# Loading three quarters of w_ch by partitions 0 to 118 and 119 to 127

## The chip, the cores and the metric

The kernel runs on one core of one Trainium2 chip. The metric is the device time of one execution in microseconds (us). The time before is the median of three runs; the profile comes from one further execution of the same kernel.

## The reference

Forgetting attention over 8 batches and 8 heads (576 positions, 64 values per head), followed by a spectral mix of its output over 64 modes and a channel mix:

```python
scores = scale * q @ k.T                                  # per batch and head
decay  = cum[:, :, :, None] - cum[:, :, None, :]          # cum = cumsum(log(clip(f)))
attn   = softmax(where(causal, -1e9, scores + decay))
x      = (attn @ v).transpose(0, 2, 1, 3).reshape(B, S, 512)

X  = np.fft.rfft(x, axis=1)                               # the first 64 modes are kept
Yr = einsum('bmd,mde->bme', Xr, w_r) - einsum('bmd,mde->bme', Xi, w_i)
Yi = einsum('bmd,mde->bme', Xr, w_i) + einsum('bmd,mde->bme', Xi, w_r)
y  = np.fft.irfft(Yr + 1j * Yi, n=S, axis=1)
u  = x + y
out = u + np.maximum(u @ w_ch, 0.0)
```

The inputs w_r and w_i are 64 x 512 x 512 in float32, 134 MB together; w_ch is 512 x 512 in float32, 1 MB.

## The kernel before, in words

The kernel has two parts, in an order written out by hand (the program order of each engine is the order of the Python statements).

The first part is the attention. A loop over 32 pairs (two heads of one batch each) turns q and k with TensorE, computes scores, masks, multiplies by v, normalises into the tile `x_all`, and takes the first 64 modes by matrix multiplication (`dft`). From the tenth pair on, each step also does one or two early portions of the spectral mix (`spec_early`) with weight tiles that are already there.

The second part begins at about 230 us. It loops over 16 groups of four modes (`u`) and the remaining row blocks (`dc`) of the weights. `spec_mms` (matmuls on L194) consumes one weight tile of 1024 KB or 512 KB at a time, `fold_modes` and `fold` (L703 to L742) bring the result back to positions, and `xw` (L690) multiplies by w_ch. After the last weight tile a closing loop (L648, L854, L902, L908) adds, applies the maximum and stores the output through SP.

Nearly all loads are issued by GpSimd (POOL) and cast from float32 to bfloat16 on the way: q and k (`load_qk`, L109, 144 KB each at the destination), v (`load_v`, L119, 288 KB, not cast), the weights (`issue_w`, L156 with 512 KB and L165 with 1024 KB) and w_ch (L322, 512 KB). They share one software queue, q0. In each pair of the first part POOL issues in a fixed order: q and k of the pair four ahead, half a weight tile, v of the pair three ahead, and usually another half of a weight tile. The weight tiles have seven buffers (`wpool`), and some early ones are lent space in `x_all` and `yx` (`guests`), so in the second part a load is issued when TensorE has consumed the tile that lay in its buffer.

The program gives the software loads eight completion counters in turn. A load waits until the load eight places before it has landed, so at most eight are in flight.

The tile `wch` has 128 partitions by 4 blocks by 512 columns. It is loaded once, in `setup_late`, which is called in pair 2; its place in POOL's order is behind the load of half a weight tile on L156 and ahead of q and k of pair 7. Its first reader is L690 at 251.8 us.

Of the kernel before, what the change touches and what calls it, by code (L numbers as in the profile page):

```python
# [17 lines left out]
def _strided(ap: bass.AP, free_dims, offset_elems: int = 0) -> bass.AP:  # L18
    new_ap = [list(ap.ap[0])] + [list(x) for x in free_dims]
    return bass.AP(tensor=ap.tensor, offset=ap.offset + offset_elems, ap=new_ap)  # L20
# [3 lines left out]
def kernel(  # L24
# [11 lines left out]
    nc = tc.nc  # L36
# [32 lines left out]
    wch = const.tile([128, NEB, D], BF16, name="wch")  # L69
# [245 lines left out]
    def setup_late():  # L315
        nc.vector.memset(XS[:, :, 24 * NM : XROW], 0.0)
        nc.vector.tensor_copy(
            perm[:].rearrange("p (b j ri) -> p b j ri", b=8, j=4),
            ident_bf[:].rearrange("p (j x ri b) -> p b j x ri", j=4, x=2, ri=2)[:, :, :, 0, :],
        )  # L320
        nc.vector.tensor_copy(rep[:], _strided(ident_bf[:, KF:128], [[0, 4], [1, KL]]))
        nc.gpsimd.dma_start(wch[:], moe_w_ch.rearrange("(eb p) e -> p eb e", p=128))  # L322

    def setup_bi(sc):
        ns = SBLK[sc]
# [226 lines left out]
    for i in range(NPAIR + 2):  # L552
# [56 lines left out]
        if i == 2:  # L609
            setup_late()  # L610
# [12 lines left out]
    with ExitStack() as bctx:  # L623
# [259 lines left out]
        for i in range(len(steps)):  # L883
# [12 lines left out]
            p, sb = steps[i][0]  # L896
# [58 lines left out]
```

## Time and profile before

| | |
|---|---|
| median of three runs | 439.38 us (439.35 to 440.37) |
| the profiled execution's own time | 440.52 us |
| its span in the profile | 438.7 us |
| mean granted TensorE clock | 0.936 |
| TensorE matmul busy | 346.3 us (79%) |
| VectorE busy | 268.2 us (61%) |
| ScalarE busy | 235.8 us (54%) |
| GpSimd busy | 133.6 us (30%) |
| bytes written by DMA | 96.75 MB, mean 221 GB/s |
| HBM read | 163.73 MB |
| the w_ch load: issue, to landing | at 32.3 us, 13.1 us |

Busy time is the time that an engine spent in instructions; it says nothing on whether the end waited for them. The chain of work that ended last, followed back from the last instruction, tells that. A "DMA" piece in it runs from the issue of a load to its landing, so it holds the time in which the load stood in its queue. The chip has 16 DMA engines that share the loads of a core, and a load has landed when the last of them has finished its part: its completion counter takes sixteen increments, whose times the trace keeps one by one.

### The profile page before, as it was taken

The page shows a single profiled execution, that of the slowest core. Times are in us where ns is not written, and L with a number is a line of the kernel's source. Part 1 is how long each engine was busy: PE and PEld are TensorE (multiplying, and loading weights), DVE is VectorE, ACT ScalarE, POOL GpSimd, SP SyncE. Part 2 cuts the span into 40 slices and gives each one's busy share as a digit, 9 for nine tenths or more (in the row PEclk, how much of TensorE's full clock was granted, in tenths as well). Part 3 has the DMA queues.
Part 4 walks back from the last instruction along what each step waited for, and adds up shares of the span by engine and source line. Part 5 has one row for each costly group of instructions (what it writes and reads, how often), then busy time and mean ns, then how long its engine had stood idle before and what let it go on. Part 6 is the DMA issues. An engine that isn't in the chain of part 4 may idle for free.

```text
span 438.7 us, 10283 instructions
## 1 busy us (share of the span) xinstructions
PE 346.3 (79%) x4285; PEld 189.7 (43%) x4285; DVE 268.2 (61%) x644; ACT 235.8 (54%) x360; POOL 133.6 (30%) x202
## 2 busy tenths in 40 slices
PE   1678787889888889888893594698986688989994
PEld 1455555555555565555551241343443233335231
DVE  6688889777877778888872221223132255465774
ACT  5657777778778666665640032033222355464874
POOL 6544444444454444444222111112021221100111
PEclk9999999999999999999997598599699699799999
DMA  9999999999999999999999999999999999994688
GB/s 192 205 234 219 230 220 230 231 227 229 233 230 223 230 223 230 223 229 224 234 212 212 212 212 212 212 211 212 212 212 211 210 209 209 211 210 83 249 299 316
DMA packets 68381, 96.75 MB, mean 221 GB/s; under 512 B 3568, under 2 KB 45040, under 8 KB 68336
## 3 DMA queue, kind: packets, MB, share of 16 engines
q0 software_dynamic: 62800, 85.64, 105.4%
q1 hardware_dynamic: 5536, 10.47, 6.6%
q8 instruction: 33, 0.54, 0.4%
q14 instruction: 12, 0.10, 0.1%
HBM read 163.73 MB, written 9.44 MB: 395 GB/s over the span
## 4 chain that ended last, share of the span: by engine, by line
DMA 39%; PE 33%; DVE 19%; ACT 4%; issue 3%; POOL 1%; DVEq 0%; POOLq 0%; ACTq 0%
DMA w<-in_moe_w_i_dram 22%; DMA w<-in_moe_w_r_dram 15%; DVE vT L384 5%; DVE x_all L492 4%; DVE qkT L360 4%; PE pav L477 4%; PE A L194 4%; PE sps L432 3%; PE tv L382 3%; PE pd L521 3%; PE vp L393 2%; PE U L648 2%; DMA qk<-in_k_dram 2%; PE Z L648 2%; DVE vn L372 2%
## 5 line engine op out<-in xcount | busy, mean ns | idle before, releaser
L439 ACT ACTIVATE et<-sps 128x1024 bf16<-128x1024 f32 x96 | 96.0, 1050 | 12.1 <-PE sps L432 9.7
L477 PE MATMUL pav<-vs,et 128*128 128x65 bf16 (+1 forms) x896 | 51.1, 196 | 0.2 <-DVE vn L372 0.2
L360 DVE COPY qkT<-tp 128x640 bf16<-128x640 bf16 x64 | 48.8, 763 | 2.5 <-PE tp L355 2.5
L804 DVE TENSOR_TENSOR Yb<-A,yx 128x512 bf16<-128x512 f32 x15 | 10.4, 691 | 64.5 <-PE A L194 64.5
L477 PEld LDWEIGHTS <-et 128*128 128x128 bf16 (+1 forms) x896 | 36.4, 101 | 17.2 <-issue 13.3
L194 PE MATMUL A<-w,XP 128*16 128x512 bf16 (+1 forms) x240 | 22.6, 457 | 25.7 <-DMA w<-in_moe_w_i_dram 15.4
L690 PE MATMUL pxw<-wch,xT 128*128 128x512 bf16 (+1 forms) x160 | 40.1, 405 | 0.0
L432 PE MATMUL sps<-qkT 64*128 64x512 bf16 (+4 forms) x320 | 38.9, 306 | 1.1 <-DVE qkT L360 1.1
L492 DVE TENSOR_TENSOR x_all<-pav,rcp 128x384 bf16<-128x384 f32 (+2 forms) x96 | 36.2, 377 | 3.3
L355 PE MATMUL tp<-ident_bf,qk 128*64 128x128 bf16 x576 | 29.3, 231 | 9.0 <-DMA qk<-in_k_dram 9.0
L384 DVE COPY vT<-tv 128x576 bf16<-128x576 bf16 x32 | 24.2, 758 | 19.2 <-PE tv L382 19.2
L697 ACT CAST XW<-pxw 128x512 bf16<-128x512 f32 (+1 forms) x16 | 9.4, 585 | 48.8 <-PE pxw L690 48.8
L156 POOL DMA_DIRECT2D w<-in_moe_w_r_dram x27 | 20.5, 759 | 40.7 <-PE A L194 9.3
L165 POOL DMA_DIRECT2D w<-in_moe_w_r_dram x16 | 11.9, 743 | 68.5 <-PE A L194 51.3
L404 ACT COPY vs<-vp 128x576 bf16<-128x576 bf16 x32 | 20.5, 640 | 21.4 <-PE vp L400 21.4
L697 ACT CAST yx<-pxw 128x512 bf16<-128x512 f32 (+1 forms) x24 | 14.0, 585 | 32.8 <-PE pxw L690 32.8
L165 POOL DMA_DIRECT2D w<-in_moe_w_i_dram x19 | 13.3, 699 | 54.8 <-PE A L194 26.3
L737 ACT CAST x_all<-pu 128x512 bf16<-128x512 f32 (+1 forms) x40 | 23.4, 585 | 12.0 <-PE pu L736 11.1
L109 POOL DMA_DIRECT2D qk<-in_q_dram x32 | 19.5, 611 | 31.8 <-PE sps L432 8.5
L491 DVE RECIPROCAL rcp<-pav 128x6 f32<-128x6 f32 (+2 forms) x96 | 16.2, 169 | 15.9 <-PE pav L477 15.8
L156 POOL DMA_DIRECT2D w<-in_moe_w_i_dram x27 | 20.3, 753 | 17.4 <-DMA w<-in_moe_w_i_dram 7.8
L372 DVE TENSOR_TENSOR vn<-vt,wn 128x576 bf16<-128x576 f32 x32 | 23.8, 745 | 2.3 <-ACT wn L297 2.3
(147 smaller groups left out, 669.9 us busy)
## 6 DMA issues: line engine op xcount, KB each, us to landing
w<-in_moe_w_r_dram POOLq DMA_DIRECT2D x16, 1024.0 KB, 29.6
w<-in_moe_w_i_dram POOLq DMA_DIRECT2D x15, 1024.0 KB, 32.4
w<-in_moe_w_r_dram POOLq DMA_DIRECT2D x27, 512.0 KB, 11.0
w<-in_moe_w_i_dram POOLq DMA_DIRECT2D x27, 512.0 KB, 12.3
vt<-in_v_dram POOLq DMA_DIRECT2D x29, 288.0 KB, 10.4
out_dram<-o_sb SPq DMA_DIRECT2D x10, 512.0 KB, 3.2
qk<-in_q_dram POOLq DMA_DIRECT2D x32, 144.0 KB, 10.9
qk<-in_k_dram POOLq DMA_DIRECT2D x32, 144.0 KB, 10.4
```

Source lines behind the costliest of these rows:

```text
L156: nc.gpsimd.dma_start(w8[:, t, :, :], src[4 * u : 4 * u + 4, dc * 128 : (dc + 1) * 128, :].rearrange("m p e -> p m e"),)
L165: nc.gpsimd.dma_start(w8[:, j : j + step, :, :].rearrange("p m r e -> p m (r e)"), src[m : m + step, 256:512, :].rearrange("m (p r) e -> p ...
L194: nc.tensor.matmul(A[32 * j : 32 * j + M, :], lhsT=lhsT, rhs=rhs, start=st_, stop=sp_)
L355: nc.tensor.transpose(tp[64 * hp : 64 * hp + 64, r - r0, :, :].rearrange("p n c -> p (n c)"), qk[:, hp, r * 64 : r * 64 + 64], ident_bf[:, :],
L360: nc.vector.tensor_copy(st[i]["T"][:].rearrange("p n (c r) -> p n c r", r=9)[:, :, :, r0:r1], tp[:, 0 : r1 - r0, :, :].rearrange("p r n c ...
L372: nc.vector.tensor_tensor(vn[:], st[i]["vt"][:], _strided(wn[:, widx(i), :], [[1, 9], [0, Dh]]), ALU.mult)
L384: nc.vector.tensor_copy(st[i]["vT"][:].rearrange("p (c r) -> p c r", r=9), tv[:].rearrange("p r c -> p c r"))
L432: nc.tensor.matmul(ps[:, hp, c : c + n], lhsT=KT[sl, jb * 128 : jb * 128 + 128], rhs=QT[sl, i0 : i0 + n], start=True, stop=True,)
L439: nc.scalar.activation(st[i]["et"][:, T, :, :], ps[:], ACT.Exp, scale=scale)
L477: nc.tensor.matmul(pav[:Ms, sb % 3, hp, :], lhsT=eblk(i, hp, jb, sb), rhs=rhs, start=(jb == 0), stop=(jb == sb),)
L492: nc.vector.tensor_tensor(x_all[:ns, g, b, lo:hi, :].rearrange("p s (h d) -> p s h d", h=2), pav[:ns, lo % 3 : lo % 3 + n, :, 0:Dh], _stri ...
L690: nc.tensor.matmul(pxw[rows, :], lhsT=xT[:, eb, sb * 128 : sb * 128 + Ms], rhs=wch[:, eb, :], start=(eb == 0), stop=(eb == NEB - 1),)
```

## The change

The block 0 of w_ch (a quarter) is loaded by one transfer of 128 partitions. The blocks 1 to 3 are loaded by two transfers, one of partitions 0 to 118 and one of partitions 119 to 127. All three are issued by GpSimd, at the place of the one before. The bytes are the same.

```diff
-        nc.gpsimd.dma_start(wch[:], moe_w_ch.rearrange("(eb p) e -> p eb e", p=128))
+        wrows = moe_w_ch.rearrange("(eb p) e -> p eb e", p=128)
+        for p0, p1, e0, e1 in ((0, 128, 0, 1), (0, 119, 1, 4), (119, 128, 1, 4)):
+            nc.gpsimd.dma_start(wch[p0:p1, e0:e1, :], wrows[p0:p1, e0:e1, :])
```

Everything else stands in the same order on every engine. As there are two more software loads, each later load uses the counter two places further on, and still waits for the load eight places before it.

## The prediction

> **What bounds the kernel now.** I first read the chain of work that ended last, in order of time, to see where the loads are on the path.
>
> ```profile
> by line: DMA w<-in_moe_w_i_dram 21.9%; DMA w<-in_moe_w_r_dram 15.1%; DVE vT L384 4.6%; DVE x_all L492 4.5%; DVE qkT L360 4.5%; PE pav L477 4.1%; PE A L194 3.7%; PE sps L432 2.9%; PE tv L382 2.9%; issue 2.8%; PE pd L521 2.7%; PE vp L393 2.4%
> ...
> 202.56 10.71 DMA w<-in_moe_w_r_dram
> 213.32 2.41 issue
> 215.74 22.35 DMA w<-in_moe_w_r_dram
> 238.13 1.13 PE A L194 x6
> 239.54 33.40 DMA w<-in_moe_w_i_dram
> ...
> 342.73 29.45 DMA w<-in_moe_w_i_dram
> 372.21 0.74 PE A L194 x6
> ```
>
> Up to 202 us the path runs over the computing engines. From there to 372.2 us it is weight loads, with one us of matmul between the landing of a tile and the issue of the next one into its buffer. Behind 372.2 us no load is on it.
>
> Next, stretches of the trace (columns: PE, PEld, DVE, ACT, POOL busy, granted clock, DMA share, GB/s written), to see whether the DMA engines ever run out of work.
>
> ```profile
> 42.00:45.00 3.00, 2.29 (x56) 1.77 (x57) 2.66 (x7) 2.37 (x4) 0.77 (x1) 1.00 1.23 206
> ...
> 372.00:378.00 6.00, 4.99 (x25) 2.27 (x25) 1.50 (x3) 1.75 (x3) 1.48 (x3) 0.55 1.17 212
> 378.00:384.00 6.00, 5.71 (x31) 2.12 (x29) 3.03 (x5) 3.65 (x7) 0.67 (x2) 0.88 1.14 210
> 390.00:396.00 6.00, 5.12 (x63) 2.44 (x61) 4.86 (x8) 2.58 (x6) 0.00 (x0) 1.00 1.14 211
> 396.00:399.00 3.00, 2.71 (x13) 1.19 (x12) 1.24 (x2) 2.24 (x5) 0.00 (x0) 1.00 0.76 143
> 399.00:402.00 3.00, 3.00 (x57) 2.09 (x54) 1.47 (x4) 0.94 (x2) 0.00 (x0) 1.00 0.43 79
> 402.00:405.00 3.00, 2.62 (x28) 1.38 (x28) 1.64 (x4) 1.02 (x3) 0.00 (x0) 1.00 0.00 0
> ```
>
> The share stays above 1 until 396 us (packets overlap) and then fades over six us: the sixteen engines do not end together. The times of the sixteen increments of a load's counter show the same. For the tile that lands at 372.17 us they lie, from the first,
>
> ```
> 0  0.20 0.26 0.35 0.67 1.38 2.03 | 3.19 3.45 3.90 4.78 5.25 5.45 5.63 5.76 5.80 us
> ```
>
> and this pattern hardly moves from tile to tile. So each DMA engine works through its own backlog without a pause, a delay that one of them once had is never made good, and a tile counts as landed when the latest engine is done. Seven engines are within 2.1 us of the first, nine are over 3.1 us behind. When the w_ch load landed (45.44 us) all were within 1.93 us. The delay grows in steps of about 1 us, on one engine at a time (4.62 to 5.69 us at the back between the tiles landing at 227.18 and 233.15 us). The DMA queues name what fits that:
>
> ```profile
> q0 software_dynamic: 62800, 85.64, 105.4%
> q1 hardware_dynamic: 5536, 10.47, 6.6%
> q8 instruction: 33, 0.54, 0.4%
> q14 instruction: 12, 0.10, 0.1%
> ```
>
> 33 instruction fetches of 16 KB took 0.4% x 16 x 438.7 / 33 = 0.85 us each. Their durations repeat with period eight, so I take it that eight engines carry them in turn, four times each by 398 us.
>
> Last, the matmul that waits for the tile landing at 372.17 us, in the order of time on PE:
>
> ```profile
> 370.03 0.65 PE L194 MATMUL A<-w,XP 128*16 128x512 bf16 x8
> 372.21 0.70 PE L194 MATMUL A<-w,XP 128*16 128x512 bf16 x8 [1.53 <-DMA w<-in_moe_w_i_dram]
> ```
>
> **The change, part by part.**
>
> *Two more issues on POOL.* At 0.75 us for the old load and 0.56 us for the small v load, the two add 1.1 to 1.5 us to an engine that is busy 30%. Cost nothing, unless POOL's order holds others up, which is next.
>
> *Waits moved.* The 119-partition load must wait for v landing at 32.76 us, the 9-partition load for the half tile landing at 35.88 us. Behind them on POOL stand q and k of pair 7 (issued at 33.29 and 36.17 us), half a weight tile (37.13) and v (38.05); they now wait for landings at 36.84, 37.49, 39.36 and 40.04 us, so they go out 1.5 to 4 us later. Who needs them: pair 7 is first turned at 55.3 us, and k landed at 46.73 us. Landing two to three us later leaves five us or more. Cost nothing on PE.
>
> *Backlog.* Three of the eight places are held by w_ch, two of them with little in them, so the backlog shrinks from about 11 us (32.34 to 43.51 us at the first engine) to 7 or 8 us for some ten loads. If an engine runs dry there, it loses that time for good. The engines with little work of w_ch are the first ones to. I count a pause of 0 to 1 us on some of them around 46 us; it costs only if it meets an engine that is later among the last. I take nothing for the forecast and keep 1 us for the range.
>
> *The bytes, engine by engine.* This is the part that can show. The old load was 2.55 us on every engine (524 KB at 206 GB/s; the first increments give 43.51 - 40.92 = 2.59 us), so three quarters are 1.91 us for 8 partitions, 0.24 us for each. No load in the trace has other than 64 or 128 partitions, both dealt equally over sixteen. Equal shares of 119 = 7 x 17 exist only on seven engines (or one), of 9 on nine. The seven then do 17 instead of 8 partitions, 9 x 0.24 = 2.2 us more, and the nine do 1 instead of 8, 1.7 us less. Dealt out in turn, the nine are the engines that the seven are not.
>
> On this the DMA page of the Trainium skill (DMA: Bandwidth & Descriptors, section "Why a DMA increments its semaphore by 16 and not by 1") gives the same deal: the largest count up to 16 that divides the slowest dimension, on consecutive engines from a cursor that goes round. No run shown so far tests it.
>
> *What it does to the end.* Which seven? If they are the early ones, the early group ends at 2.03 + 2.2 = 4.2 us and the late one at 5.80 - 1.7 = 4.1 us, so every tile of the last hundred us lands 5.8 - 4.2 = 1.6 us sooner. If a late engine is among the seven, its tiles land 2.2 us later. These are the two ends, -1.6 and +2.2 us, before PE has its say.
>
> PE's say: at 372.21 us PE had waited 1.53 us. Its work before reaches back without another load wait to 342.24 us, where it waited 4.21 us, so that starts 1.6 us sooner as well; about half of this is lost because the clock is at half there until 348.8 us. PE then still waits about 0.8 us at the new 370.6 us. The work behind it starts 1.6 us sooner at a full clock (the clock drops at 372.7 us) and nothing waits for a load up to the end; the last tile lands at 402.26 us against its use at 403.4 us, and both move. So the end moves by 1.6 us.
>
> **Forecast:** the profiled execution had 440.52 us, of which the span is 438.7; 1.6 us less is 438.9. The median of the three runs is 1.14 us below the profiled one, and I take the step off that: 439.38 - 1.6 = 437.8 us. A measurement of this kernel tells about 0.3% (1.3 us) from no change.
>
> **The rivals.**
>
> *The late engines get the 119 (slower).* The trace does not name engines. If the fetches lie on the half that the 119-partition load begins with, at least one engine with 5.2 to 5.8 us of delay takes 2.2 us more. The tile at 372.17 us lands at 374.3. From 372.7 to 379.5 us the clock is at half (0.55 in the stretch from 372), so a wait there costs half of itself: 1.3 us if the clock keeps its times, 2.2 us if it moves along, 440.7 to 441.6, say 441.2 us. It decides as soon as any engine over 4 us behind is among the seven. For it: a consecutive block of seven that misses all nine late ones has only one place. Against: the late ones are nine and the early ones seven, which is just the split of a deal in turn if eight engines with fetches and one neighbour are its second part. I judge 58 to 22 between these, and it is a judgement.
>
> *The 119 go out as eight per engine (no change).* Fourteen engines keep 8, one has 7, one none, and the 9 go singly to nine engines: nine engines +0.24 us, one -1.9 us. The latest engine moves by 0 to +0.24 us unless it is the one relieved, and the next (5.76 us) is 0.04 us behind it: 439.4 us, within 0.3 us. For it: it keeps all sixteen busy as every row of the trace does. Chance 0.13.
>
> By the same section of the Trainium skill some direct copies from GpSimd are dealt just so, rounded up over sixteen engines, and no row here tells whether a casting load is one of these.
>
> *An engine of the second group runs dry (less gain).* The gain falls from 1.6 to about 0.6 us, 438.8 us. For it: the smaller backlog above. Against: the early engines had a lead of 5 us on 11 us of backlog at 200 us and did not run dry. Chance 0.07.
>
> **How the numbers follow.** Forecast 0.58, slower rival 0.22, even deal 0.13, dry engine 0.07. The forecast's own range is 437.0 to 438.5 us (a step of the clock's timing is worth some 0.8 us either way); 0.05 of it lies within 0.3%. The even deal may relieve a late engine that leads the pack (0.02), the dry engine may lose less (0.03). So faster 0.58 - 0.05 + 0.02 + 0.03 = 0.58; within 0.3% 0.05 + 0.11 + 0.04 = 0.20; slower 0.22. The range of 8 in 10 reaches from the forecast's low side to the middle of the slower rival, 436.8 to 441.2 us.
>
> **What would show it.** Right: sixteen increments of late tiles within some 4.3 us instead of 5.8, DMA share fading over 4 us, the last tile landing 1.6 us sooner, the matmul of 372.21 us at about 370.6. Wrong: a pattern with one engine at 7 us or more and the same matmul near 374 us (late engines took the 119); the old pattern (even deal); a DMA share below 1.1 around 46 us (dry); q or k of pair 7 waited for at 55 us (my cover failed).

## The result and the profile after

The changed kernel takes 441.63 us (median of seven runs, 440.87 to 444.19) against 439.67 us of the kernel before (median of seven runs, 439.35 to 440.37). The ratio is 1.0042, with a 95% interval of 1.0024 to 1.0059: 1.0 to 2.6 us slower, where 1.6 us faster was forecast. The profiled execution took 441.34 us, with a span of 439.6 us; that of before took 440.52 us, above its own median, so the two profiles differ by less than the medians do.

First the page of the kernel after, the chain that ended last, by engine and by line.

```profile
DMA 42%; PE 28%; DVE 19%; issue 6%; ACT 3%; POOL 1%; DVEq 0%; POOLq 0%
DMA w<-in_moe_w_r_dram 26%; DMA w<-in_moe_w_i_dram 12%; DVE vT L386 5%; DVE x_all L494 4%; DVE qkT L362 4%; PE pav L479 4%; PE A L194 3%; PE sps L434 3%; PE tv L384 3%; PE pd L523 3%; DMA vt<-in_v_dram 3%; PE vp L395 2%; DVE vn L374 2%; DMA qk<-in_k_dram 2%; PE Z L650 2%
```

The weights are still the largest item. The same chain in order of time (start, length, what) shows a difference at its end.

```profile
354.75 29.45 DMA w<-in_moe_w_r_dram
384.48 19.72 DMA w<-in_moe_w_i_dram
405.42 0.86 PE pywl L876 x4
```

Before, the last load on the path landed at 372.2 us. Now the very last tile is on it: issued at 384.48, landed at 404.19 us. PE in order of time (start, length, and in brackets the idle time with what ended it) shows both places.

```profile
371.71 0.65 PE L194 MATMUL A<-w,XP 128*16 128x512 bf16 x8
374.20 0.66 PE L194 MATMUL A<-w,XP 128*16 128x512 bf16 x8 [1.84 <-DMA w<-in_moe_w_i_dram]
...
404.24 0.40 PE L211 MATMUL AT<-XP,w 128*128 128x16 bf16 x8 [0.40 <-DMA w<-in_moe_w_i_dram]
```

The matmul of 372.21 us starts at 374.20, which the prediction named as the sign that late engines took the 119 partitions. Next the stretches at the end (columns as before: PE, PEld, DVE, ACT, POOL, clock, DMA share, GB/s).

```profile
372.00:378.00 6.00, 3.08 (x32) 1.41 (x25) 1.70 (x3) 1.64 (x4) 1.08 (x2) 1.00 1.19 210
...
396.00:399.00 3.00, 2.71 (x13) 1.04 (x11) 1.48 (x3) 2.23 (x5) 0.00 (x0) 1.00 1.06 199
399.00:402.00 3.00, 2.86 (x54) 1.82 (x53) 1.25 (x3) 0.72 (x2) 0.00 (x0) 1.00 0.59 109
402.00:405.00 3.00, 2.24 (x26) 0.88 (x22) 1.44 (x4) 0.61 (x2) 0.00 (x0) 1.00 0.13 24
```

From 396 us on the DMA shares are close to those of two us earlier in the kernel before (1.05, 0.67 and 0.23 in 394:397, 397:400 and 400:403). The increments of the last tile tell it more exactly: the first came 1.93 and the last 1.94 us later, so the fading of the engines moved back as a whole and kept its length. The granted clock in 372 to 378 us is 1.00, against 0.55 before, so PE made up there for part of the late tile in this execution. The matmul on the last tile started at 403.37 us before and starts at 404.24 us now; these 0.87 us are the difference of the two spans (439.6 against 438.7 us).

The same view around the w_ch loads, and below it one stretch of the kernel before.

```profile
42.00:45.00 3.00, 2.29 (x58) 1.67 (x55) 2.66 (x6) 2.78 (x3) 1.10 (x2) 1.00 1.24 201
45.00:48.00 3.00, 2.53 (x32) 1.73 (x31) 2.38 (x11) 1.56 (x4) 0.11 (x1) 1.00 1.23 222
48.00:51.00 3.00, 2.64 (x63) 1.80 (x60) 2.66 (x7) 2.82 (x4) 2.59 (x4) 1.00 0.93 164
51.00:54.00 3.00, 2.18 (x26) 1.50 (x25) 2.40 (x9) 1.51 (x4) 1.81 (x4) 1.00 1.16 223
```

```profile
48.00:51.00 3.00, 2.17 (x54) 1.67 (x55) 2.66 (x7) 2.63 (x3) 0.60 (x1) 1.00 1.21 216
```

In one stretch the share falls to 0.93 and the rate to 164 GB/s, against 1.21 and 216: some engines ran dry. What held the loads up is in POOL's order of time.

```profile
32.89 0.54 POOL L324 DMA_DIRECT2D wch<-in_moe_w_ch_dram  x1 [1.72 <-DMA x_all<-in_moe_w_i_dram]
33.58 1.07 POOL L324 DMA_DIRECT2D wch<-in_moe_w_ch_dram  x1 [0.15 <-issue]
36.48 0.60 POOL L324 DMA_DIRECT2D wch<-in_moe_w_ch_dram  x1 [1.82 <-DMA w<-in_moe_w_r_dram]
...
44.50 0.60 POOL L109 DMA_DIRECT2D qk<-in_k_dram  x1 [0.35 <-DMA wch<-in_moe_w_ch_dram]
48.41 0.75 POOL L156 DMA_DIRECT2D w<-in_moe_w_r_dram  x1 [3.31 <-DMA wch<-in_moe_w_ch_dram]
```

Eight places behind the 119-partition load stands half a weight tile. It waits 3.31 us for that load and is issued at 48.41 us. In the kernel before it was issued at 42.82 us, after another wait:

```profile
42.82 0.77 POOL L156 DMA_DIRECT2D w<-in_moe_w_r_dram  x1 [1.73 <-DMA yx<-in_moe_w_r_dram]
```

Last, the sixteen increments, from the first, of the 119-partition load (42.23 to 48.13 us) and of the tile that lands at 374.16 us:

```
119 partitions   0 .03 .27 .30 .34 .34 .65 2.18 2.42 | 3.47 3.69 3.70 3.73 3.95 4.12 5.90 us
tile at 374.16   0 .12 .19 .92 1.35 1.76 1.91 | 2.91 2.95 3.01 3.08 3.13 4.42 5.65 5.85 5.89 us
```

Seven engines stand out in the first row. The second row is as wide as before (5.89 against 5.80 us), but its first increment is 1.89 us and its last 1.99 us later.

### The profile page after: what moved, and what is told of

It is laid out like the page before. It is cut to its first block, busy times and chain, and to the rows that moved or that the text cites. A ratio compares the mean times of both kernels' runs of the same rounds, so it can differ in the third digit from the quotient of the medians.

```text
span 439.6 us, 10285 instructions
## 1 busy us (share of the span) xinstructions
PE 342.9 (78%) x4285; PEld 188.3 (43%) x4285; DVE 267.9 (61%) x644; ACT 235.8 (54%) x360; POOL 134.8 (31%) x204
## 4 chain that ended last, share of the span: by engine, by line
DMA 42%; PE 28%; DVE 19%; issue 6%; ACT 3%; POOL 1%; DVEq 0%; POOLq 0%
DMA w<-in_moe_w_r_dram 26%; DMA w<-in_moe_w_i_dram 12%; DVE vT L386 5%; DVE x_all L494 4%; DVE qkT L362 4%; PE pav L479 4%; PE A L194 3%; PE sps L434 3%; PE tv L384 3%; PE pd L523 3%; DMA vt<-in_v_dram 3%; PE vp L395 2%; DVE vn L374 2%; DMA qk<-in_k_dram 2%; PE Z L650 2%
## 5 line engine op out<-in xcount | busy, mean ns | idle before, releaser
L165 POOL DMA_DIRECT2D w<-in_moe_w_i_dram x19 | 13.3, 698 | 55.9 <-PE A L194 38.2
L109 POOL DMA_DIRECT2D qk<-in_k_dram x32 | 19.6, 611 | 21.7 <-DMA w<-in_moe_w_i_dram 6.8
```

The lines of the kernel that those rows point to most:

```text
L109: nc.gpsimd.dma_start(qk[64 * n : 64 * n + 64, :, :], src[b, 2 * g : 2 * g + 2, :, :].rearrange("h (p r) d -> p h (r d)", p=64),)
L165: nc.gpsimd.dma_start(w8[:, j : j + step, :, :].rearrange("p m r e -> p m (r e)"), src[m : m + step, 256:512, :].rearrange("m (p r) e -> p ...
```

## The experiments

Three theories were open. By the first, three loads in place of one cost the time: their issues, their waits, their places among the eight in flight. By the second, the uneven deal costs it, because engines that are late anyway are among the seven heavy ones. By the third, the engines that ran dry cost it. The heavy engines of a load were read off its increments: that choice of seven out of sixteen which, with one common delay for the seven, turns the increments of the load before into those of the load after best. The number seven is not put in: in each of the nine kernels with two or three blocks of 119 partitions, six or eight heavy engines fit worse (root mean square error 0.17 to 0.39 us) than seven (0.03 to 0.15 us). An engine is called late below when it stands over 2.5 us behind the first one.

**Three loads, dealt evenly.** 112 and 16 partitions in place of 119 and 9.

```diff
-        for p0, p1, e0, e1 in ((0, 128, 0, 1), (0, 119, 1, 4), (119, 128, 1, 4)):
+        for p0, p1, e0, e1 in ((0, 128, 0, 1), (0, 112, 1, 4), (112, 128, 1, 4)):
```

> Blocks 1 to 3 of w_ch are split at partition 112 instead of 119 (112 = 16 x 7 and 16 = 16 x 1), so there are still three loads on the same three places, but equal shares exist on all sixteen DMA engines. Theory A (the 119 partitions go to seven engines; the load eight places behind waits for the slowest of them and the other nine run dry): no uneven load, no dry spell, the increments of the second load lie within 2.5 us of each other instead of 5.9, the time is that of the kernel before, 439.4 to 440.0 us. Theory B (only the deal counts: a late engine is among the seven): the same, 439.4 to 440.0 us. Theory C (three places in the window of eight instead of one are what costs): as slow as the changed kernel, 441 to 442 us.

Measured 439.6 us (12 runs; the kernel before, measured with it, 439.77 us), ratio 0.9996, interval 0.9984 to 1.0008. No seven engines stand out: the increments of the second load lie within 1.69 us. The half tile eight places behind it went out at 45.36 us. So three loads, their places and their waits cost nothing that the measurement can tell, and the theory of issues, waits and places falls.

**The order of the two reversed.** The 9 partitions first, at the place of the change.

```diff
-        for p0, p1, e0, e1 in ((0, 128, 0, 1), (0, 119, 1, 4), (119, 128, 1, 4)):
+        for p0, p1, e0, e1 in ((0, 128, 0, 1), (119, 128, 1, 4), (0, 119, 1, 4)):
```

> The two loads of blocks 1 to 3 change places: first the 9 partitions, then the 119. If the engines are dealt in turn, the nine engines of the small load come first and the seven of the large one are others than in the changed kernel. Theory A (dry spell of the nine light engines, whichever they are): the increments of the 119-partition load spread by some 5 to 6 us again, the half weight tile eight places behind it is held up, the time is 441 to 442 us as with the changed kernel. Theory B (a late engine among the seven is what costs, and without one the late tiles come 1.6 us sooner): the time differs from the changed kernel's by over 1 us if the new seven hold no late engine (438 to 439 us), and is 441 to 442 us if they hold one too. Theory C: as the changed kernel, 441 to 442 us.

Measured 443.31 us (six runs, 441.36 to 445.95), ratio 1.0074, interval 1.0045 to 1.0104. The last tile landed at 406.75 us, 4.5 us behind that of the kernel before. The last increments of the loads stood 2.6 us behind those of before just after w_ch and 4.4 us behind at 190 us; the first ones were up to 0.8 us ahead at first, lost that by some 80 us and were 4.7 us behind at 190 us. The first loss is about what the prediction gave for a heavy late engine (2.2 us). The later growth of the first increments falls on two stretches in which the DMA share dips again (1.17 at 108 to 114 and 1.10 at 180 to 186 us, against 1.21 and 1.22 before), so engines ran dry there a second and a third time; what the last increments lost after 50 us the runs do not settle.

**The whole load, late.** One load of w_ch in the last pair, where eight large loads are in flight.

```diff
-        nc.gpsimd.dma_start(wch[:], moe_w_ch.rearrange("(eb p) e -> p eb e", p=128))
...
+        if i == NPAIR - 1:
+            wrows = moe_w_ch.rearrange("(eb p) e -> p eb e", p=128)
+            for p0, p1, e0, e1 in ((0, 128, 0, 4),):
+                nc.gpsimd.dma_start(wch[p0:p1, e0:e1, :], wrows[p0:p1, e0:e1, :])
```

> The w_ch load, in one transfer of 128 partitions as before the change, is issued in the last pair (about 222 us), where loads of 1024 KB are queued and the backlog is 15 to 30 us. It is the reference for the split load at the same place. All theories: the same bytes, 439 to 440.5 us; the first reader at about 252 us may have to wait for it for up to 1 us.

Measured 440.29 us (12 runs), ratio 1.0004, interval 0.9990 to 1.0018; the last tile landed at 402.84 us. The place in itself costs nothing that the measurement can tell.

**The split, late.** The three loads of the change at that place.

```diff
-            for p0, p1, e0, e1 in ((0, 128, 0, 4),):
+            for p0, p1, e0, e1 in ((0, 128, 0, 1), (0, 119, 1, 4), (119, 128, 1, 4)):
```

> The three loads of the changed kernel (128, 119 and 9 partitions) at the place of the last pair, where no engine can run dry behind a backlog of 15 to 30 us. To be compared with the whole load at that place. Theory A (the dry spell costs): none here, so at most the deal is left: the light engines end 1.7 us sooner, the heavy seven 2.2 us later, and the time is between 1.6 us below and 2.2 us above the whole load, by which engines are late. Theory B (a late engine among the seven, nothing else): 2 us above the whole load. Theory C (places in the window): as the whole load, since nothing waits for the window there.

Measured 441.27 us (12 runs), ratio 1.0034, interval 1.0022 to 1.0046, 0.98 us over the late whole load by the medians. For the late whole load and then the late split, the PE line of the matmul that started at 372.21 us in the kernel before, and the line ahead of it (view as above):

```profile
370.98 0.65 PE L194 MATMUL A<-w,XP 128*16 128x512 bf16 x8
372.81 0.65 PE L194 MATMUL A<-w,XP 128*16 128x512 bf16 x8 [1.19 <-DMA w<-in_moe_w_i_dram]
```

```profile
372.21 0.64 PE L194 MATMUL A<-w,XP 128*16 128x512 bf16 x8
373.97 0.65 PE L194 MATMUL A<-w,XP 128*16 128x512 bf16 x8 [1.12 <-DMA w<-in_moe_w_i_dram]
```

The tile comes 1.16 us later. Nothing ran dry here (DMA share 1.16 at 234 to 240 us, 1.15 with the late whole load), and the increments show the bare deal. Ahead of the 119-partition load, after it, and at the last tile:

```
w_r tile at 235.64   0 .01 .06 .50 .64 .68 .85 | 3.02 3.46 3.49 3.73 4.00 4.29 4.47 4.65 5.75 us
119 partitions       0 .40 .54 | 3.49 3.64 3.76 3.77 3.90 4.32 4.50 4.52 4.65 5.69 | 6.75 7.15 7.95 us
last tile at 403.97  0 .43 .57 | 3.43 3.47 4.10 4.31 4.47 4.55 4.87 5.46 5.68 5.75 | 7.01 8.01 8.82 us
```

Seven early engines became three: four of them joined the group at 3.4 to 5 us, and three late ones went out to 7 us and more. The best choice has the heavy seven at 0, 0.08, 0.67, 0.86, 3.07, 3.52 and 4.33 us, and a gap of 3.7 us between heavy and light. The first engine gained 1.70 us against the late whole load and the last one lost 1.13 us. The theory of the late engines holds, without any dry engine.

**The start of the deal moved.** A load of a few partitions by 8 elements, into a tile that nothing reads, goes ahead of the late split's three, so that the 119 should fall on other engines. In four kernels it had 4, 8, 12 or 3 partitions; in a fifth nothing was added and the order was reversed as above, so that the 9 partitions came first.

```diff
+    step = const.tile([16, 8], BF16, name="step")
...
+            nc.gpsimd.dma_start(step[0:4, :], moe_w_ch[0:4, 0:8])
             for p0, p1, e0, e1 in ((0, 128, 0, 1), (0, 119, 1, 4), (119, 128, 1, 4)):
```

> As the late split (441.27 us), but a load of 4 partitions x 8 elements into a tile that nothing reads goes out ahead of its three, so that the deal of the 119 begins four engines further on: engines 4 to 10 of the turn do 17 partitions a block instead of 0 to 6. Theory G (the late engines stand together in the turn, so some start of the deal meets seven early ones): one of the three turned kernels shows the heavy seven all below 3.1 us and its late tiles land 1.2 to 1.7 us before those of the late whole load (402.84 us), about 439 us. Theory I (late engines are mixed with early ones all round the turn, so every seven in a row hold at least three late ones): each of the three has its late tiles 0.6 to 2.3 us behind the late whole load and a time of 440.9 to 442.5 us, at this start too. If a place in the turn meant nothing, the increments would look as in the late split.

> The same with a load of 8 partitions x 8 elements first: the 119 lie on engines 8 to 14 of the turn, six of which had 8 partitions a block less one of the nine light ones in the late split. Theory G: last tile at 401.2 to 401.7 us and about 439 us if these are the early ones. Theory I: last tile 403.4 to 405.1 us, time 440.9 to 442.5 us.

> The same with a load of 12 partitions x 8 elements first: the 119 lie on engines 12 to 15 and 0 to 2 of the turn. Theory G: last tile at 401.2 to 401.7 us and about 439 us if these are the early ones. Theory I: last tile 403.4 to 405.1 us, time 440.9 to 442.5 us.

Measured 441.04, 441.35 and 441.51 us (12 runs each; before 439.78 us). None of these starts met seven early engines, which fits theory I and not G, as far as the starts were the intended ones. The two odd starts were then to tell an order from none.

> As the late split (441.27 us) with the 9 partitions ahead of the 119, so that the 119 lie on engines 9 to 15 of the turn. The four even starts (0, 4, 8, 12) each met three late engines and four of the others. Theory I2 (the eight engines with instruction fetches are every second one of the turn): a seven that begins at an odd place holds four late engines and three others, so the load's pattern is made by adding 3.84 us to three increments under 3 us and four over 3 us; the four early ones left stay within about 1 us of the first; last tile 403.4 to 405.1 us, time 441 to 442 us. Theory M (mixed without order): three and four, or another split, by chance; the same time.

> As the late split with a load of 3 partitions x 8 elements first, into a tile that nothing reads: the 119 lie on engines 3 to 9 of the turn. Theory I2: again an odd start, so four late and three early engines are among the heavy seven, and four early ones are left near the first. Theory M: any split. Last tile 403.4 to 405.1 us, time 441 to 442 us in both.

Measured 441.70 us (seven runs) and 441.07 us (ten runs; before 440.02 us). All six late splits together, with the heavy engines' delays before the load and the landing of the last tile:

| late split | heavy engines stood at (us behind the first) | last tile, us | ratio to before (interval) |
|---|---|---|---|
| no extra load | 0, .08, .67, .86, 3.07, 3.52, 4.33 | 403.97 | 1.0034 (1.0022 to 1.0046) |
| 4 partitions first | 0, .13, .65, .66, 3.06, 3.42, 3.65 | 403.34 | 1.0024 (1.0011 to 1.0037) |
| 8 first | .01, .58, .89, 2.87, 3.68, 3.88, 4.92 | 404.79 | 1.0028 (1.0013 to 1.0043) |
| 12 first | .41, .76, .90, 1.16, 3.11, 3.75, 3.83 | 403.62 | 1.0034 (1.0020 to 1.0049) |
| 9 of w_ch first | .47, 3.29, 3.31, 4.08, 4.17, 4.38, 6.04 | 404.88 | 1.0037 (1.0023 to 1.0051) |
| 3 first | 0, .72, .77, 1.44, 3.31, 3.44, 3.49 | 403.46 | 1.0025 (1.0011 to 1.0038) |

Neighbours within one group (3.49 and 3.65, say) cannot be told apart by this reading; the number in each group can. Every seven held three to six late engines (with 8 partitions first four, not the three that a later expectation counts for it), and every one made the kernel slower. The order I2, every second engine late, falls: it asked for four late ones at both odd starts, and they had six and three. Starts of 8 and 9 places should differ by one engine at most and differ by more, so either the late engines or the start of the deal were not the same in each execution; which of the two, the increments do not tell. The instruction fetches speak for the start: their durations follow each other in one order of eight in all fourteen traces (893, 893, 949, 945, 936, 975, 974 and 961 ns, single longer ones aside) and begin at another place of it in each, which is what the same eight engines, taken in turn, would give. That is a sign and no proof.

**One block split.** At the place of the change three blocks go whole and one as 119 and 9 partitions.

```diff
-        for p0, p1, e0, e1 in ((0, 128, 0, 1), (0, 119, 1, 4), (119, 128, 1, 4)):
+        for p0, p1, e0, e1 in ((0, 128, 0, 3), (0, 119, 3, 4), (119, 128, 3, 4)):
```

> At the place of the change, three blocks go whole and one block as 119 and 9 partitions: a third of the uneven bytes, nearly the same number of loads. Theory of the dry spell (the nine light engines lose their gain because the half tile eight places behind the 119-partition load is held up until their backlog is gone): with a third the load behind is held up by 0.7 us only, nobody runs dry, the light engines keep -0.57 us and the heavy ones have +0.72 us; first increments of late tiles 0.3 to 0.6 us before the even split's, last ones 0.3 to 0.7 us behind, time 0.2 to 0.6 us over the kernel before. Rival (the loss at this place goes in proportion to the bytes dealt unevenly, no threshold): first increments +0.3 to 0.6 us and last ones +0.6 us, as a third of the changed kernel's, time 0.6 us over.

Measured 440.12 us (12 runs; before 439.78), ratio 1.0006, interval 0.9992 to 1.0021. It was meant as a smaller dose and was none: over the 119-partition load the first increment moved by 0.64 and the last by 0.42 us, and no group parted. Neither theory was tested, but something else had shown; the same form was run at the late place.

> At the late place, three blocks whole and one block as 119 and 9 partitions. In the early run of this form the 119-partition load of one block moved all sixteen increments by about the same time (first +0.64, last +0.42 us) and no group stood out. Theory F (the deal goes by the form of the access: one block is a contiguous piece of the matrix and is dealt evenly, three blocks are dealt on seven engines): the sixteen increments keep their pattern to 0.15 us over the 119-partition load but for one or two engines, last tile within 0.3 us of the late whole load (402.84), time 440.0 to 440.6 us. Rival (the deal is on seven engines here too and the early run hid it): seven increments move 1.28 us more than nine, last tile 0.3 to 0.7 us behind, time 440.5 to 441.0 us.

Measured 439.84 us (ten runs; before 440.02), ratio 0.9994, interval 0.9982 to 1.0006; the last tile landed at 402.40 us. Ahead of the 119-partition load and after it:

```
three blocks     0 .02 .10 .17 .62 .67 .76 2.40 3.31 3.55 3.78 3.84 4.07 4.16 4.41 6.00 us
119 partitions   0 .03 .09 .16 .28 .59 .71 2.38 3.32 3.50 3.75 3.79 4.05 4.14 4.40 5.91 us
```

Theory F: one block was dealt evenly. The issue on POOL tells the forms apart, too. For the late split, this kernel and the two-block kernel below, the three w_ch issues with their durations (ns, shortest/median/longest; from and to, us):

```profile
L563 POOL DMA_DIRECT2D wch<-in_moe_w_ch_dram x3: 551/603/1068, 217.7 to 220.1; - x3
```

```profile
L563 POOL DMA_DIRECT2D wch<-in_moe_w_ch_dram x3: 527/575/746, 216.3 to 218.1; - x3
```

```profile
L324 POOL DMA_DIRECT2D wch<-in_moe_w_ch_dram x3: 582/698/978, 32.6 to 36.1; - x3
```

Three blocks of 119 partitions took 1.07 us to issue, two blocks 0.98 us; no issue of the one-block kernel took over 0.75 us.

**Two blocks split.** The dose again, with a form that is dealt on seven engines.

```diff
-        for p0, p1, e0, e1 in ((0, 128, 0, 1), (0, 119, 1, 4), (119, 128, 1, 4)):
+        for p0, p1, e0, e1 in ((0, 128, 0, 2), (0, 119, 2, 4), (119, 128, 2, 4)):
```

> At the place of the change, two blocks whole and two as 119 and 9 partitions: two thirds of the uneven bytes, three loads as before. By the theory of the deal on seven engines, heavy ones 2.72 us over the 119-partition load against light ones 0.16 us, a gap of 2.56 us at once (3.84 in the changed kernel). Theory of the dry spell: the light engines are held up by 1.4 us where the changed kernel holds them up by 2.2, they keep part of their gain: first increments of late tiles 0 to 1.3 us behind those of the kernel before, last ones +0.8 to +1.5, time 440.3 to 441.0 us. Proportional rival: first and last both +1.3 us (two thirds of 1.94), time 441.0 us. If two blocks are dealt evenly as one was: increments as in the even split (+0.55 us both), time within 0.3 us of before.

Measured 441.15 us (12 runs; before 440.02), ratio 1.0032, interval 1.0014 to 1.0050; the time is just above what was expected. The best choice of seven gives a gap of 2.4 us. The stretch in which the changed kernel ran dry:

```profile
48.00:51.00 3.00, 2.23 (x58) 1.67 (x55) 2.66 (x7) 2.72 (x3) 1.65 (x3) 1.00 1.18 219
```

The share stays at 1.18. By 60 us the first increments are 0.4 us earlier than with the even split, where the changed kernel has them 1.3 us later, and at the last tile they are 0.2 us ahead of the kernel before; the proportional rival asked for 1.3 us behind, the theory of the dry spell for 0 to 1.3. So the dry stretch came with three blocks and not with two. Yet the last increment of the last tile is 1.12 us late and the time is up: an uneven deal costs here with hardly an engine dry. This distance to the kernel before swings on the way, as the fetches delay the engines in an order that begins elsewhere in each execution: the last increments are at most 0.3 us behind from 233 to 352 us and 1.1 to 1.2 us behind from the tile of 357 us on, when 30 of the 33 fetches have fallen.

## Why the prediction was wrong, point by point

*The path.* Right, and it is why the deal shows: weight loads bound the second part, and PE follows the latest engine tile by tile.

*Two more issues and the moved waits.* Right. The three issues took 0.54 + 1.07 + 0.60 us against 0.75, 1.46 us more; k of pair 7 landed at 49.34 us (46.73 before) and was turned at 55.80 us without a wait. The even split shows the sum of all that: nothing that can be told.

*The bytes, engine by engine.* Right in kind and nearly in size. Three blocks of 119 partitions went to seven engines. The gap to the other nine was estimated at 2.2 + 1.7 = 3.9 us (16 partitions by 0.24 us), and read as 3.5 to 3.9 us in the late splits and 3.1 us in the changed kernel. The section of the Trainium skill that the prediction cites (DMA: Bandwidth & Descriptors, "Why a DMA increments its semaphore by 16 and not by 1") has the same deal; the traces agree with it for two and three blocks.

*Which seven.* This is the step that failed: "If they are the early ones", with 58 to 22 for it. The heavy seven of the changed kernel stood, when the load came, at 0.26 to 0.88 us and one at 2.57 us behind the first. Being early at 42 us says little: the delays of about one us come one engine at a time until 398 us, and which engines were the heavy ones can no longer be read at the end, since the pause at 49 us mixed the groups. In the six late splits, where most delays had fallen already, the heavy seven held three to six late engines each. Two blocks at the place of the change, with hardly a pause, show the same loss there (last tile 1.12 us later than before). A split into seven and nine in the trace was taken for the split into seven and nine of the deal; no run shows a tie between the two.

*The end.* With a late engine among the seven the prediction had tiles 2.2 us later. The tile at 372.17 us came 1.99 us later, the last tile 1.94 us. Part of that may be scatter: the last tile of the five kernels without an uneven deal (before, even split, late whole, both one-block kernels) landed between 402.26 and 402.84 us, 402.58 in the mean. The seven kernels with three blocks dealt on seven engines, the reversed early one left out, have 403.34 to 404.88, 404.04 in the mean, so 1.5 us is the better number (1.8 us with the reversed one and its 406.75).

*The backlog.* This step failed, too. "A pause of 0 to 1 us on some of them around 46 us", taken as nothing, was a pause of about two us: the engine that was first finished k at 49.29 us and its part of the next half tile at 53.65 us, 4.36 us later, where the even split needed 2.31. The cause is the half tile held until 48.41 us, and it was in reach: a load that waits for the load eight places before it waits for the slowest engine of that load, while the others go on emptying what they have. The light engines lost their gain of 1.0 us by this and came out 1.3 us behind the even split. By these numbers the forecast would have failed at this place even if all seven heavy engines had stayed early: light engines with later delays would have been the last ones, later than before. No run shows that case. How much of the 1.9 us at the last tile is owed to the pause cannot be told apart at the end: heavy and light engines are both late by then. The late split loses without it (ratio 1.0034 against 1.0042, with intervals that overlap), two blocks nearly without it (1.0032).

*PE's say* was not put to the test, since nothing came sooner. The cover it counted on for the last tile was thin: 1.1 us before, and PE now waits 0.40 us there.

*The rivals.* The slower one was right in its main step, a late engine among the seven, and nearly in time: matmul at 374.3 us (374.20 measured) and 441.2 us (441.63). That the time came so near is in part luck: it gave the pause to another rival, and it took its price from PE at half clock, where the profiled execution had the full clock at 372 to 378 us and lost its 0.87 us at the last tile. Its sign of one engine at 7 us or more did not come in the changed kernel, because the pause pulled the light engines back to the rest; without the pause it did (8.82 us). The even deal came true for another form, one block. The dry engine came too, but on the light engines and at more than the 1 us it was given.

## What to carry to other kernels

Where loads bound a kernel, a tile lands with its latest engine, so a load whose partition count has no even deal over the sixteen engines is a bet on which engines are late, and a pattern of increments does not name them. Look at how each load is dealt, keep partition counts even over the engines, and count an uneven deal as its full extra share on the latest engine unless a trace shows which engine takes what. Where a window of loads is in flight, look also for the load that waits for the slow one: the other engines' backlog must outlast that wait.

## What the runs showed of the hardware

- The same 119 partitions are dealt in two ways. Two or three blocks of a row went to seven engines (gaps of 2.4 and 3.1 to 3.9 us); one block, a contiguous piece of the matrix, was dealt evenly (no group; at the place of the change first +0.64 and last +0.42 us), at both places. Whether its being contiguous or its having no dimension for the blocks decides that, no run tells. The section of the Trainium skill that the prediction cites (DMA: Bandwidth & Descriptors, "Why a DMA increments its semaphore by 16 and not by 1") has an exception for some direct copies from GpSimd, rounded up over sixteen engines; the one-block load fits that, though it casts.
- From the issue of the held half tile at 48.41 us to the start of its transfer on the first engine there were about 2.9 us (landing at 53.65 us, less the 2.31 us that the same transfer took with the even split). By that, a load here must be issued some three us before an engine runs empty, or the engine pauses.
- The delays of an engine are never made good, but they can be evened out at a price: in the changed kernel the spread fell from 5.90 us at the 119-partition load to 2.52 us ten loads later, because the first engines paused.
- An issue on POOL took longer where the load was dealt on seven engines: 1.07 us for three blocks and 0.98 us for two, against 0.75 us for the whole w_ch of 128 partitions and 0.72 us at most for the loads of the even split.
